# Zero products spread over the weight blocks, keys cast and transposed first in a step, and one copy for transposed keys: a change to a fused retention and feed-forward kernel

## The chip, the cores and the metric

The kernel runs on one core of a Trainium2 chip. The core has a matrix engine (TensorE, in the profile PE, with its weight loads as PEld), three engines that work on elements (VectorE or DVE, ScalarE or ACT, GpSimd or POOL), a sync engine (SP) that issues most transfers, and 16 DMA engines that carry them. The metric is the device time of one execution in microseconds; lower is better.

## What is computed

The reference has two stages. The first is a recurrence over 768 positions for 4 batches and 8 heads with head size 64, in which a state of 64x64 per head decays and takes up one outer product per position:

```python
for t in range(S):
    state = gamma * state + einsum('bhd,bhe->bhde', k[:, :, t], v[:, :, t])
    y[:, :, t] = scale * einsum('bhd,bhde->bhe', q[:, :, t], state)
x = y.transpose(0, 2, 1, 3).reshape(B * S, H * D)      # 3072 x 512
a, b = x @ w1, x @ w2                                   # 512 -> 1024
out = (a * b @ w3) @ w_out                              # 1024 -> 1024 -> 512
```

The inputs and the output are float32. The kernel computes its products in fp16 with sums in float32, and it folds w3 @ w_out into one matrix of 1024x512 before it needs it.

## The kernel before

**Tiles and steps.** The sequence is cut into chunks of 128 positions. One step handles one chunk of two batches, that is 256 rows of x; there are 12 steps (NSTEP = 12, numbered 0 to 11). Steps 0 and 1 are handled in another arrangement (pairs of positions), step 2 has its own function `step2` (line 844), and steps 3 to 11 run through `step(m)` (line 874). In each step, for all heads:

- `scores` (line 374) multiplies the transposed keys kT and the queries into psA, 32 small products; VectorE masks them into `am` (line 389).
- `intra` (line 521) multiplies `am` with the values into psY, and `inter` (line 590) adds the queries times the carried state.
- `kv` (line 537) multiplies keys and values into psK. VectorE adds the carried state to it (lines 572 and 564), and GpSimd decays the sum (line 565) to the state of the next chunk.
- `outputs_back` (line 606) scales psY into the tile `xt`, which is the input x of the feed-forward stage (line 613).

The class `Ffn` (line 621) holds the feed-forward stage. `ab(f)` makes one block of 128 of the 1024 hidden columns: eight products of 128x256 on TensorE (line 635), a copy of the first half's result by ScalarE (`pa`, line 644), and its product with the second half by VectorE (`ht`, line 650). `o_unit(e)` makes 128 output rows: eight products of 512 columns (line 660), a scaling by ScalarE into `osb` (line 664), and a store issued by the sync engine (line 666).

The stages are staggered. Step m computes the scores and the key-value products of chunk m, the outputs of chunk m-2 and the hidden columns of chunk m-1.

**What sets the order.** The schedule is written out by hand: each engine runs its instructions in the order in which the program emits them, and waits come only from data and from buffers. Transfers from the sync engine are one queue. The eight semaphores of this queue are taken in turn, so a transfer also waits until the transfer eight issues before it has landed. Buffers come from pools: the products of the feed-forward stage, psK and some transposes share four banks with the tag psF, `osb` has four buffers, kT two, k16 three.

**How the keys come.** `load_k(m)` (line 87) brings them into a staging tile, and is called two steps ahead. `k_cast` (line 295) turns them into fp16 in two halves, in `step` both on GpSimd (line 303). There are two ways to transpose them. `k_dma` (line 361) has the sync engine issue one transposing DMA from k16 to kT, for the keys of steps 5, 7, 8, 10 and 11. `k_transposes` (line 349) does it with eight products against an identity matrix on TensorE (line 357), for the keys of steps 2, 3, 4, 6 and 9; the result stands in one bank, and `cast_to` (line 216) copies one half to kT on VectorE (line 218) and the other on ScalarE (line 220). K_PE = (3, 5, 8) names the steps that prepare keys in this second way within `step`.

**The order within a step.** After `scores`, `inter` and `outputs_back` for the two sides, `step` emits the state's additions and decay (`kv_backs`), the masks (`am_back`), the first output unit with its store, then the key cast and the transposing DMA for the next step, then the second output unit with its store, and then the loads for later steps. The hidden columns, the value cast (`v_cast`, line 310) and, in even steps, the query casts and their transposing DMAs (`q_dma`, line 336) follow.

**The head.** At the start TensorE folds w3 and w_out block by block: `cast_w3` (line 227) casts a block of w3 as it lands, `w3_transpose` (line 240) transposes it with eight products and VectorE copies the result, `cast_wo` (line 222) casts a block of w_out on ScalarE and GpSimd, and `w3_part(f, i)` (line 250) adds two products of 512 columns per pair of blocks. `busy(m, tag, n)` (line 677) issues m products of a zero matrix with n columns (512 if none is given) whose result nobody reads; the kernel before does this eight times at the start and ten times with 84 columns after the first transposes.

Of the kernel before, what the change touches and what calls it, by code (L numbers as in the profile page):

```python
# [18 lines left out]
def kernel(  # L19
# [11 lines left out]
    nc = tc.nc  # L31
# [5 lines left out]
    NSTEP = (B // 2) * NCH  # L37
# [4 lines left out]
    K_PE = 4  # L42
# [173 lines left out]
    def cast_to(dst, src, on_dve):  # L216
        if on_dve:
            nc.vector.tensor_copy(dst, src)
        else:
            nc.scalar.copy(dst, src)  # L220

    def cast_wo(i):
        dst = WO[i][:, :, :].rearrange("p a n -> p (a n)")
        nc.scalar.copy(dst[:, 0:512], wo_st[i][:, 0:512])  # L224
        nc.gpsimd.tensor_copy(dst[:, 512:1024], wo_st[i][:, 512:1024])

    def cast_w3(f):
        t = att.tile([128, 1024], HP, tag="qT", name="w3h", bufs=5)
        st = w3_st[f]
        if f < 4:  # L230
            nc.vector.tensor_copy(t[:, 0:512], st[:, 0:512])  # L231
            nc.scalar.copy(t[:, 512:1024], st[:, 512:1024])
        else:
            cast_to(t[:, :], st[:, :], f == 4)
        W3h[f] = t

    def bank(tag, shape, dtype, name):
        return ps_at.tile(shape, dtype, tag=tag, name=name)

    def w3_transpose(f):  # L240
        src, ps = W3h.pop(f), bank(("X0", "X1")[f % 2], [128, 1024], HP, "psW3")
        for g in range(8):
            c0 = (g // 2) * 256 + g % 2
            nc.tensor.transpose(  # L244
                ps[:, g * 128 : (g + 1) * 128], src[:, c0 : c0 + 255 : 2], ident16[:, :]
            )
        w3t[f] = att.tile([128, 1024], HP, tag="k16" if f < 3 else "v16", name="w3t", bufs=3)
        nc.vector.tensor_copy(w3t[f][:, :], ps[:, :])  # L248

    def w3_part(f, *parts):  # L250

        for i in parts:
            for r in range(2):
                g = i * 2 + r
                nc.tensor.matmul(  # L255
                    acc[f], lhsT=w3t[f][:, g * 128 : (g + 1) * 128], rhs=WO[i][:, r, :],
                    start=(g == 0), stop=(g == 7),
                )
            if i == 3:
                cast_to(W3O[f][:, :], acc[f], f < 3)  # L260
# [19 lines left out]
    def q_cast(n, *engs):  # L280
        if n not in q_in:
            return
        q16s[n] = att.tile([128, 1024], HP, tag="q16", name="q16", bufs=2)
        pairs_cast(q16s[n], q_in.pop(n), *engs)
# [10 lines left out]
    def k_cast(m, engs):  # L295
        k16 = att.tile([128, 2, 512], HP, tag="k16", name="k16", bufs=3)
        k32 = k_in.pop(m)
        if len(engs) == 1:
            parts = [(k16[:, :, :].rearrange("p e x -> p (e x)"), k32[:, :, :].rearrange("p e x -> p (e x)"))]
        else:  # L300
            parts = [(k16[:, e, :], k32[:, e, :]) for e in range(2)]
        for eng, (dst, src) in zip(engs, parts):
            (nc.scalar.copy if eng is nc.scalar else eng.tensor_copy)(dst, src)  # L303
        k16s[m] = k16
# [40 lines left out]
    def new_kT(m):  # L345
        kTs[m] = att.tile([128, 2, NP, 128], HP, tag="kT", name="kT", bufs=2)
        return kTs[m]

    def k_transposes(m, tag, on_dve):
        k16, kT = k16s[m], new_kT(m)  # L350
        if tag:
            ps = bank(tag, [128, 2, NP, 128], HP, "psTk")
        else:
            ps = ps_f.tile([128, 2, NP, 128], HP, tag="psF", name="psTk")
        for e in range(2):
            for p in range(NP):
                nc.tensor.transpose(ps[:, e, p, :], k16[:, e, p * 128 : (p + 1) * 128], ident16[:, :])  # L357
        for e in range(2):
            cast_to(kT[:, e, :, :], ps[:, e, :, :], on_dve[e])

    def k_dma(m):
        nc.sync.dma_start_transpose(
            new_kT(m)[:, :, :, :].rearrange("p e a j -> p (e a) j"),
            k16s[m][:, :, :].rearrange("p e x -> p (e x)"),
        )
# [8 lines left out]
    def scores(m, engs=None):  # L374
        kT = kTs.pop(m)
        am = att.tile([128, 2, NP * 2, L], HP, tag="am", name="am")
        ps = [bank(f"X{r}", [128, NP * 2, L], FP, "psA") for r in range(2)]
        for e in range(2):
            for p in range(NP):
                for r in range(2):  # L380
                    for s in range(2):
                        nc.tensor.matmul(  # L382
                            ps[r][half(s), p * 2 + e, :], lhsT=kT[half(r), e, p, half(s)],
                            rhs=queries(m, e, p, s, r), start=True, stop=True,
                        )
        AMs[m] = am

        def back(r):
            nc.vector.tensor_tensor(  # L389
                am[:, r, :, :], ps[r][:, :, :],  # L390
                keep[:, :].unsqueeze(1).broadcast_to((128, NP * 2, L)), MULT,
            )

        return back
# [282 lines left out]
    def busy(m, tag="Y0", n=512):  # L677
        if tag:
            ps = bank(tag, [128, 512], FP, "psZ")
        else:  # L680
            ps = ps_f.tile([128, 512], FP, tag="psF", name="psZ")
        for _ in range(m):
            nc.tensor.matmul(ps[:, 0:n], lhsT=Z[:, 0:128], rhs=Z[:, 0:n], start=True, stop=True)
# [3 lines left out]
    acc = [ps_f.tile([128, DM], FP, tag="psF", name="psW")[:, :] for _ in range(4)]  # L687
    w3_transpose(0)
    cast_wo(0)
    busy(10, n=84)  # L690
    w3_part(0, 0)
    cast_w3(1)
    w3_transpose(1)
    cast_wo(1)
    w3_part(0, 1)
    w3_part(1, 0, 1)
    cast_w3(2)
    w3_transpose(2)
    cast_wo(2)
    w3_part(0, 2)  # L700
    w3_part(1, 2)
# [80 lines left out]
    def four_banks():  # L782
        return [ps_f.tile([128, 2, TB], FP, tag="psF", name="psF")[:, :, :] for _ in range(4)]
# [9 lines left out]
    ps = four_banks()  # L793
# [24 lines left out]
    ps = four_banks()  # L818
# [19 lines left out]
        f1.ab(f)  # L838
    q_transposes(3, "Y0", False)
    stores = [f0.o_unit(0, store=False)]  # L840
    k_transposes(2, "Y1", (True, False))
    f1.ab(2)

    def step2():
        am_back = scores(2)
        am_back(0)
        am_back(1)
        stores.append(f0.o_unit(1, store=False))
        k_cast(3, (nc.gpsimd, nc.scalar))
        for n in (4, 5):  # L850
            q_cast(n, nc.gpsimd)
        for n in (4, 5):
            q_dma(n)
        for store in stores:
            store()
        for f in range(3, 5):
            f1.ab(f)
        intra(2)
        kv_back = kv(2, True)
        kv_back(0)  # L860
        f1.ab(5)
        k_transposes(3, None, (True, False))
        f1.ab(6)
        kv_back(1)
        v_cast(3, (nc.gpsimd, nc.gpsimd))
        f1.ab(7)
# [5 lines left out]
    K_PE = (3, 5, 8)  # L872

    def step(m):

        kv_backs = []
        if m > 4:
            last = None if m in EARLY else ended(intra(m - 1))
            if m < NSTEP:
                kv_backs.append(kv(m, True))  # L880
                am_back = scores(m)
            inter(m - 1, last)
        else:
            inter(m - 1)
            if m == 4:
                kv_backs.append(kv(m, True))
            am_back = scores(m)
        outputs_back(m - 1, 0)
        outputs_back(m - 1, 1)
        if m >= NSTEP:  # L890
            return
        for kv_back in kv_backs:
            kv_back(0)
            kv_back(1)
        am_back(0)
        am_back(1)
        ffn[m - 2].o_unit(0)
        if m + 1 < NSTEP:
            k_cast(m + 1, (nc.gpsimd, nc.gpsimd))
            if m not in K_PE:  # L900
                k_dma(m + 1)
        ffn[m - 2].o_unit(1)
        load_q(m + 3) if m % 2 == 0 else None
        load_k(m + 2)
        load_v(m + 2)
        load_q(m + 3) if m % 2 else None
        for f in range(2):
            ffn[m - 1].ab(f)
        if m + 1 in EARLY:
            intra(m)  # L910
        if m + 1 < NSTEP:
            v_cast(m + 1, (nc.gpsimd, nc.gpsimd))
        if m == 3:
            intra(m)
            kv_back = kv(m)
            kv_back(0)
        ffn[m - 1].ab(2)
        ffn[m - 1].ab(3)
        if m == 3:
            kv_back(1)  # L920
        if m % 2 == 0:
            for n in (m + 2, m + 3):
                q_cast(n, nc.gpsimd)
            for n in (m + 2, m + 3):
                q_dma(n)
        for f in range(4, 8):
            if f == 6 and m in K_PE:
                k_transposes(m + 1, None, (True, False))
            ffn[m - 1].ab(f)

    step2()
# [40 lines left out]
```

## Time and profile before

| | us |
|---|---|
| median of 4 runs | 186.42 |
| lowest and highest | 185.82, 187.53 |
| the profiled execution | 186.32 |
| its span in the profile | 184.30 |
| TensorE busy | 174.8 (95%) |
| VectorE, ScalarE, GpSimd busy | 108.2, 74.5, 70.2 |
| products of the hidden columns (L635) | 672 of 128x256, 77.0 busy |
| products of the output units (L660) | 200, 43.7 busy |

The profile is one execution. Its page gives busy times by engine and by groups of instructions; other views give each engine's instructions in order of time, and for each idle time the instruction whose end released the waiting one. In a line of a timeline the first number is the start in us from the start of the span, the second the time from the first instruction's start to the last one's end, then engine, line, operation, output<-input by the program's names, shape and count; what stands in brackets is the idle time before it and its releaser. Products on TensorE overlap: a product that lasts 0.38 us alone follows its neighbour at a shorter pitch, so that a run of them lasts the count minus one times the pitch plus one whole duration. A row of SPq is the time that the sync engine took to issue a transfer; the transfer lands later.

### The profile page before, as it was taken

To read this page: it belongs to the slowest core of one execution; us is meant where nothing else is said; L and a number is where in the kernel's file an instruction comes from. 1 tells how busy PE (TensorE), PEld (TensorE's weight loads), DVE (VectorE), ACT (ScalarE), POOL (GpSimd) and SP (SyncE) were. 2 spreads that over 40 slices of the span, in tenths; PEclk is the share of its full clock that TensorE was granted. 3 is DMA by queue.
4 is the path that set the end of the run, shared out by engine and by line. 5 is a ranking of instruction groups with operands and counts; after the bars stand their busy time and mean duration, and the time that the engine had idled before them with its cause. 6 is when DMAs were issued, how large, how long until landed. Compare 5 with 4: busy or idle time off the path is not lost.

```text
span 184.3 us, 6239 instructions
## 1 busy us (share of the span) xinstructions
PE 174.8 (95%) x2642; PEld 125.2 (68%) x2642; DVE 108.2 (59%) x205; ACT 74.5 (40%) x161; POOL 70.2 (38%) x126
## 2 busy tenths in 40 slices
PE   7789979999989999999999999899999999999992
PEld 2545546688556785885967858669678587685872
DVE  1447667642559659648467584395585855846330
ACT  3445735655641342433344424233344242342532
POOL 3228355853447660924407365028253090000000
PEclk9999999999999999999999999999999999999999
DMA  6999999997899999999998999999998932200203
GB/s 210 406 413 391 292 289 358 410 351 178 179 250 233 191 268 215 241 270 211 157 253 199 241 221 205 188 240 275 195 134 215 190 80 68 105 9 13 104 0 114
DMA packets 78474, 39.44 MB, mean 214 GB/s; under 512 B 56304, under 2 KB 72944, under 8 KB 78448
## 3 DMA queue, kind: packets, MB, share of 16 engines
q1 hardware_dynamic: 78016, 38.54, 86.5%
q8 instruction: 20, 0.33, 0.8%
q10 hardware_dynamic: 432, 0.52, 0.8%
q14 instruction: 6, 0.05, 0.1%
HBM read 29.36 MB, written 6.29 MB: 193 GB/s over the span
## 4 chain that ended last, share of the span: by engine, by line
PE 60%; DMA 22%; SPq 9%; POOL 3%; ACT 2%; issue 1%; ACTq 0%; DVE 0%
PE psF L635 34%; PE psO L660 20%; SPq L63 9%; DMA stg<-in_k_dram 8%; DMA stg<-in_moe_w_out_dram 4%; DMA stg<-in_moe_w_dram 4%; DMA stg<-in_v_dram 3%; DMA kT<-k 3%; PE psY L598 2%; PE psY L530 2%; PE psA L382 1%; PE psK L550 1%; PE psTk L357 1%; POOL v L310 1%; ACT osb L664 1%
## 5 line engine op out<-in xcount | busy, mean ns | idle before, releaser
L635 PE MATMUL psF<-xt,w 128*128 128x256 f16 x672 | 77.0, 273 | 0.0
L635 PEld LDWEIGHTS <-w 128*128 128x128 f16 x704 | 68.2, 98 | 10.3
L650 DVE TENSOR_TENSOR ht<-pa,psF 128x256 f16<-128x256 f32 x88 | 36.9, 420 | 38.6 <-PE psF L635 21.8
L660 PE MATMUL psO<-w3o,ht 128*128 128x512 f16 (+2 forms) x200 | 43.7, 371 | 0.0
L644 ACT COPY pa<-psF 128x256 f32<-128x256 f32 x80 | 29.7, 372 | 33.8 <-PE psF L635 33.8
L660 PEld LDWEIGHTS <-ht 128*128 128x128 f16 x200 | 18.5, 98 | 19.7
L664 ACT ACTIVATE osb<-psO 128x512 f32<-128x512 f32 (+2 forms) x25 | 14.5, 580 | 41.4 <-PE psO L660 41.4
L613 DVE TENSOR_TENSOR xt<-psY,YS 64x512 f16<-64x512 f32 (+1 forms) x29 | 21.1, 727 | 5.7 <-PE psY L598 5.4
L310 POOL TENSOR_TENSOR v<-stg,VS 128x512 f16<-128x512 f32 x20 | 20.5, 1042 | 5.6 <-DMA stg<-in_v_dram 5.6
L565 POOL TENSOR_TENSOR t<-s,GS 128x512 f16<-128x512 f32 x8 | 8.3, 1039 | 37.2 <-DVE s L564 37.2
L290 POOL CAST q<-stg 128x1024 f16<-128x1024 f32 (+1 forms) x12 | 12.0, 1003 | 16.2 <-DMA stg<-in_q_dram 11.9
L389 DVE TENSOR_TENSOR am<-psA,keep 128x512 f16<-128x512 f32 x20 | 12.8, 680 | 0.7 <-PE psA L382 0.7
L303 POOL CAST k<-stg 128x512 f16<-128x512 f32 x18 | 10.7, 612 | 1.4 <-DMA stg<-in_k_dram 1.3
L255 PE MATMUL psW<-wo,w3t 128*128 128x512 f16 x32 | 7.8, 380 | 1.6 <-ACT wo L224 1.5
L787 PE MATMUL psF<-xt,w 128*128 128x256 f16 x64 | 8.5, 274 | 0.2
L248 DVE COPY w3t<-psW 128x1024 f16<-128x1024 f16 x8 | 5.5, 689 | 5.3 <-PE psW L244 5.3
L269 PE MATMUL psW<-wo,w3t 128*128 128x512 f16 x32 | 8.4, 381 | 0.0
L787 PEld LDWEIGHTS <-w 128*128 128x128 f16 x64 | 5.8, 98 | 2.0 <-ACT w L220 0.6
L572 DVE TENSOR_TENSOR t<-psK,t 128x512 f16<-128x512 f32 x9 | 6.2, 689 | 0.7 <-PE psK L550 0.5
L244 PEld LDWEIGHTS <-w3h 128*128 128x128 f16 x64 | 4.4, 103 | 3.0 <-DVE w3h L231 1.6
L382 PE MATMUL psA<-qT,kT 64*64 64x64 f16 x320 | 5.0, 195 | 1.4 <-DMA kT<-k 0.9
L255 PEld LDWEIGHTS <-w3t 128*128 128x128 f16 x32 | 3.0, 98 | 4.6 <-issue 1.7
(91 smaller groups left out, 150.4 us busy)
## 6 DMA issues: line engine op xcount, KB each, us to landing
stg<-in_moe_w_dram SPq DMA_DIRECT2D x16, 512.0 KB, 8.7
stg<-in_q_dram SPq DMA_DIRECT2D x12, 512.0 KB, 6.5
out_dram<-osb SPq DMA_DIRECT2D x22, 256.0 KB, 3.7
stg<-in_k_dram SPq DMA_DIRECT2D x20, 256.0 KB, 5.5
stg<-in_v_dram SPq DMA_DIRECT2D x20, 256.0 KB, 5.9
stg<-in_moe_w_out_dram SPq DMA_DIRECT2D x4, 512.0 KB, 6.8
stg<-in_k_dram SPq DMA_DIRECT2D x2, 512.0 KB, 10.1
stg<-in_v_dram SPq DMA_DIRECT2D x2, 512.0 KB, 8.9
```

Source lines behind the costliest of these rows:

```text
L63: nc.sync.dma_start(dst, src)
L255: nc.tensor.matmul(acc[f], lhsT=w3t[f][:, g * 128 : (g + 1) * 128], rhs=WO[i][:, r, :], start=(g == 0), stop=(g == 7),)
L290: (nc.scalar.copy if eng is nc.scalar else eng.tensor_copy)(dst[:, :].rearrange("i (t h d) -> i h t d", t=2, d=D)[:, hs, :, :], src[:, :]. ...
L310: eng.tensor_tensor(v16[:, e, :].rearrange("j (h d) -> j h d", d=D), v32[:, e, :].rearrange("j (h d) -> j h d", d=D), VS[:, 2, :].unsqueez ...
L389: nc.vector.tensor_tensor(am[:, r, :, :], ps[r][:, :, :], keep[:, :].unsqueeze(1).broadcast_to((128, NP * 2, L)), MULT,)
L613: nc.vector.tensor_tensor(XT[m][to, :, s, :].rearrange("p (a e) (i t) -> p a e t i", e=2, t=2), psYs[m][s][fr, :, :].rearrange("p (a e) (t ...
L635: nc.tensor.matmul(ps[:, :], lhsT=W[d][:, f * 128 : (f + 1) * 128], rhs=self.x(d), start=(d == 0), stop=(d == 3),)
L644: nc.scalar.copy(self.pa[f][:, :], ps[:, :])
L650: nc.vector.tensor_tensor(self.HT[:, f, :], self.pa.pop(f)[:, :], ps[:, :], MULT)
L660: nc.tensor.matmul(psO[:, :], lhsT=self.HT[:, f, e * 128 : (e + 1) * 128], rhs=W3O[f][:, cs], start=(f == 0), stop=(f == 7),)
L664: nc.scalar.activation(osb[:, cs], psO[:, :], AF.Copy, scale=final_scale)
L787: nc.tensor.matmul(ps[f // 2][:, f % 2, :], lhsT=W[d][:, f * 128 : (f + 1) * 128], rhs=f0.x(d), start=(d == 0 and f % 2 == 0), stop=(d == ...
```

## The change

It has three parts.

1. In the head, ten zero products of 84 columns after the first transposes become two of 400 columns. Three zero products of 512 columns are added after `w3_part(0, 0)`, three more after `w3_transpose(1)`, and two of 400 columns after `w3_transpose(2)`.
2. `k_transposes` copies the transposed keys with one VectorE copy of 1024 columns instead of one copy of 512 on VectorE and one on ScalarE.
3. In `step`, the key cast on GpSimd and, where the step is not in K_PE, the transposing DMA of the next step's keys move from behind the first output unit to right behind `outputs_back`. On GpSimd the cast is now ahead of the state's decay (L565); on the sync engine the transposing DMA is ahead of the first output unit's store. ScalarE, VectorE and TensorE keep their order apart from parts 1 and 2.

The parts of the diff (the same edit of the two other calls of `k_transposes` is left out):

```diff
-    def k_transposes(m, tag, on_dve):
+    def k_transposes(m, tag):
...
-        for e in range(2):
-            cast_to(kT[:, e, :, :], ps[:, e, :, :], on_dve[e])
+        nc.vector.tensor_copy(
+            kT[:, :, :, :].rearrange("p e a j -> p (e a j)"), ps[:, :, :, :].rearrange("p e a j -> p (e a j)")
+        )
...
     w3_transpose(0)
     cast_wo(0)
-    busy(10, n=84)
+    busy(2, n=400)
     w3_part(0, 0)
+    busy(3)
     cast_w3(1)
     w3_transpose(1)
+    busy(3)
     cast_wo(1)
     w3_part(0, 1)
     w3_part(1, 0, 1)
     cast_w3(2)
     w3_transpose(2)
+    busy(2, n=400)
     cast_wo(2)
     w3_part(0, 2)
...
-    k_transposes(2, "Y1", (True, False))
+    k_transposes(2, "Y1")
...
         outputs_back(m - 1, 1)
         if m >= NSTEP:
             return
+        if m + 1 < NSTEP:
+            k_cast(m + 1, (nc.gpsimd, nc.gpsimd))
+            if m not in K_PE:
+                k_dma(m + 1)
         for kv_back in kv_backs:
             kv_back(0)
             kv_back(1)
         am_back(0)
         am_back(1)
         ffn[m - 2].o_unit(0)
-        if m + 1 < NSTEP:
-            k_cast(m + 1, (nc.gpsimd, nc.gpsimd))
-            if m not in K_PE:
-                k_dma(m + 1)
         ffn[m - 2].o_unit(1)
```

More of the change, by code (lines that the diff above doesn't have):

```diff
@@ L861, in step2 @@
         f1.ab(5)
-        k_transposes(3, None, (True, False))
+        k_transposes(3, None)
         f1.ab(6)
@@ L927, in step @@
             if f == 6 and m in K_PE:
-                k_transposes(m + 1, None, (True, False))
+                k_transposes(m + 1, None)
             ffn[m - 1].ab(f)
```

## The prediction

> **What bounds the kernel now.** I read the page first, then the list of waits of TensorE, then the chain, then the engines' timelines around each wait.
>
> ```profile
> span 184.3 us, 6239 instructions
> PE 174.8 (95%) x2642; PEld 125.2 (68%) x2642; DVE 108.2 (59%) x205; ACT 74.5 (40%) x161; POOL 70.2 (38%) x126
> ...
> PE psW L255 <- ACT wo L224: 1.5, 2, 0.8
> PE psTq L328 <- DVE k L290: 1.2, 1, 1.2
> PE psA L382 <- DMA kT<-k: 0.9, 1, 0.9
> PE psA L382 <- ACT kT L220: 0.4, 1, 0.4
> PE psTq L328 <- POOL q L290: 0.3, 1, 0.3
> PE psW L244 <- DVE w3h L231: 0.2, 1, 0.2
> ```
>
> TensorE is busy for 95% of the span, and its work runs in one fixed order, so only two things change the time: a change of TensorE's own work after the head, or a change of the waits. The waits (total us, times, longest) are few. Three belong to the weight stage before 13 us, one (1.2) sits at 24.12, and 0.3, 0.4 and 0.9 come after it. From 24 us on, a wait saved moves the end; before 24.12, a wait saved or added is taken up by the 1.15 us that TensorE idles there until a key load has landed and been cast.
>
> **Part 1, zero products between the first blocks.** The head, TensorE alone (start, us, then count after the x):
>
> ```profile
> 1.27 3.60 PE L683 MATMUL psZ<-zeros 128*128 128x512 f16 x8 [1.27 <-DVE zeros L143]
> 4.85 1.04 PE L244 MATMUL psW<-ident,w3h 128*128 128x128 f16 x8
> 5.68 0.91 PE L683 MATMUL psZ<-zeros 128*128 128x84 f16 x10
> 6.68 0.64 PE L255 MATMUL psW<-wo,w3t 128*128 128x512 f16 x2
> 7.50 0.62 PE L244 MATMUL psW<-ident,w3h 128*128 128x128 f16 x8 [0.19 <-DVE w3h L231]
> 8.93 1.45 PE L255 MATMUL psW<-wo,w3t 128*128 128x512 f16 x6 [0.81 <-ACT wo L224]
> 10.22 0.61 PE L244 MATMUL psW<-ident,w3h 128*128 128x128 f16 x8
> 11.49 1.46 PE L255 MATMUL psW<-wo,w3t 128*128 128x512 f16 x6 [0.66 <-ACT wo L224]
> ```
>
> The eight first products have a pitch of (3.60-0.63)/7 = 0.42 us (one alone lasts 0.63); the six at 8.93 have (1.45-0.38)/5 = 0.214 (one alone 0.38). The eight transposes shrink from 1.04 to 0.62. So TensorE doubled its rate between 5.7 and 7.5, although the page's granted clock reads 1.00 throughout: this row of the page does not show the early half rate.
>
> Ten products of 84 columns go (slow pitch (0.91-0.28)/9 = 0.07, together 0.70) and two of 400 come (0.42x400/512 = 0.33 each, 0.66): equal, and both lie in the time until w3_part(0,0) may start at 6.68. Three of 512 follow w3_part(0,0): 6.68+2x0.214 = 7.11, so they end at 7.75, and w3_transpose(1) starts 0.25 later than 7.50. Behind it wait its copy on VectorE (8.16, now about 8.43 to 9.12) and the parts of row 1. The next three run from 7.75+8x0.055 = 8.19 to 8.83, inside the 0.81 gap that ends at 8.93 with ScalarE's cast of W_out; w3_part(0,1) is not delayed, and w3_part(1) at 9.36 finds its copy done (9.12). The last two of 400 run from 10.66 to 10.99, inside the gap ending at 11.49. In all 1.61 us of zeros in 1.66 us of gaps (0.19+0.81+0.66). Cost 0; nothing gained either, since loads and casts set 8.93 and 11.49. Without that cover the price is the zeros' own time less the 1.15 at 24.12.
>
> [...] The trace has one moment, before 7.5. By the row the cost is 0. [...]
>
> **Part 2, one copy for the transposed keys.** Step 2's first keys (VectorE, then ScalarE, then TensorE):
>
> ```profile
> 50.30 0.42 DVE L218 COPY kT<-psTk 128x512 f16<-128x512 f16 x1 [2.27 <-PE psTk L357]
> 50.89 0.59 ACT L220 COPY kT<-psTk 128x512 f16<-128x512 f16 x1
> 50.77 0.32 PE L382 MATMUL psA<-qT,kT 64*64 64x64 f16 x16
> 51.53 0.32 PE L382 MATMUL psA<-qT,kT 64*64 64x64 f16 x16 [0.44 <-ACT kT L220]
> ```
>
> ScalarE's half is late, behind an output's scaling. The single 1024-wide copy has an exact row (a kT copy at 24.78: 0.69). It starts at 50.30 as now and ends 50.99, so all 32 scores start at about 51.04. The scores of later steps take 0.31 from first to last start, plus 0.1 to the next product: 51.45, where the output's products start at 51.78 now. Gain 0.33.
>
> The same copy in steps 2 (k3), 3, 5 and 8 adds 0.69-0.42 = 0.27 to VectorE and takes 0.58 from ScalarE. VectorE is tightest after 56.25, where it runs on without a gap to 61.56: xt is done at 60.5 for 60.24 (read at 61.32) and the masked scores at 61.83 for 61.56 (read at 63.07). Cover 0.8 and 1.2, cost 0. Elsewhere it idles 0.4 between products. In step 5 the bank of the transposes is now freed by VectorE (92.04+0.69 = 92.73; its next product comes at 93.33: no wait), and the second state bank waits for VectorE instead of for ScalarE's last pa (ends 93.78 after being pushed back by its kT copy). That third psK product now goes at 93.83 for 93.70: gain 0.13.
>
> **Part 3, cast and transposing DMA first in the step.** What happens in step 7 now (sync queue):
>
> ```profile
> 107.49 4.81 SPq L340 DMA_TRANSPOSE qT<-q  x2
> 112.39 0.53 SPq L666 DMA_DIRECT2D out_dram<-osb  x1
> 113.02 1.28 SPq L362 DMA_TRANSPOSE kT<-k  x1
> 114.40 0.54 SPq L666 DMA_DIRECT2D out_dram<-osb  x1
> ...
> 118.72 0.45 PE L382 MATMUL psA<-qT,kT 64*64 64x64 f16 x32 [0.90 <-DMA kT<-k]
> ```
>
> The keys' DMA lands 5.66 after issue, 0.9 late. The least gain is the swap with one store: issue at 112.40, landing 118.06, and 0.28 of the wait stays (gain 0.62). But the same move in step 6 acts first. There the casts stand on GpSimd behind the state product L565, which waits for VectorE until 98.0; so the kT issue is at 100.18, the second store at 101.51, and the loads behind it start at 102.09. The keys of step 7 were issued by 91.7 and take 4.7 (median of the two): 96.4, when GpSimd idles (7.93 before L565). Casts (1.17) to 97.6, kT issue (1.23) to 98.8, both stores to 99.9: the loads of step 6 start 2.1 earlier. Then step 7's q transposes shift from 107.49 to 105.4 and end at 110.3, kT is issued there, and it lands at 113.4 to 116.0 (3.1, the median landing, to 5.7). Needed at 117.82. I take the full 0.90.
>
> What it costs: two casts pass L565, so L565 (1.04) ends up to 1.2 later, 111.0 for 109.83 in step 7; its result is next read by L572 at 121.76. The value casts behind are not passed. On the sync queue kT passes one store (256 KB, 0.5 to issue), which starts up to 1.5 later; its osb is one of four, two per step, so it is reused two steps (24 us) later. If a key load landed late, GpSimd, the sync queue, the stores and the loads behind them would wait for it: in step 4 the keys, issued by 69.7 and landing 5.4 later, are cast by 75.4 to 76 as now. Steps 3, 5 and 8 have no kT DMA and their casts pass only GpSimd's L565.
>
> [...]
>
> **Sum.** 0.33+0.13+0.90 = 1.36. The profiled execution took 186.32 (span 184.30 and 2.02 around it): 184.96. It lies 0.10 under the median 186.42, so 185.1. Unknown: at 131.2 TensorE loses 0.25 to ScalarE's mark in step 9, whose release no view explains; 0 to 0.25 gain, I take 0, because the mark waits for TensorE and not for the copy.
>
> **Rivals.**
> A (0.60): as summed, 184.6 to 185.6.
> B (0.20): the wait for keys stays or moves. [...] then 0.9 is not saved and only 0.46 is: 186.0. Against it: 1.8 us of room even at the slowest landing.
> C (0.12): more goes: the 0.25 at 131.2, 0.27 at 47.47, and longer waits in the slower of the four runs (187.53): about 184.3.
> D (0.08), slower: [...] Then the zeros cost 6x0.42+0.66 = 3.2, TensorE has no gaps to hide them, and 3.2-1.15 = 2.0 reaches the end: 188.4 without, about 187.1 with the gains. It decides once the zeros' excess passes 1.15, so for a doubling after about 10 us. Against it: the trace has it before 7.5, and the four runs lie within 1.7.
>
> **Numbers.** 185.1 is A's. The range 184.3 to 186.7 holds A, B and most of C, and leaves D's bad end out. One per cent of 186.42 is 1.86, about what a measurement can tell from no change: faster than 184.56 is C and A's lowest end, 0.15; slower than 188.28 is D's bad half, 0.05; the rest 0.80.
>
> **What would show it.** Right: no wait of psA for kT by DMA or ScalarE; the kT issue of step 7 before 111 and landed before 117; step 6's loads at about 100; the psK after step 5 within 0.3 from first to last start; w3_part(0,1) at 8.9 and (0,2) at 11.5 with zeros filling the gaps. Wrong: w3_part(0,2) after 12, products of 0.42 pitch past 8, a gap at 24.12 that has vanished, GpSimd waiting for a key load with the sync queue standing still, or psF waiting on VectorE's kT copy.

## The result, and the profile after

| | before | after |
|---|---|---|
| median, us | 186.45 (58 runs) | 184.57 (39 runs) |
| lowest and highest | 185.16, 189.86 | 183.65, 187.00 |
| the profiled execution, us | 186.32 | 184.69 |
| its span, us | 184.30 | 182.7 |

After against before on the same chips: 0.9904, interval 0.9886 to 0.9921. That is 1.79 us less (1.47 to 2.13, taken from 186.45). The sum had 1.36, a ratio of 185.1/186.42 = 0.9929: the sign, the place and most of the size were right, and the gain is somewhat larger than forecast; 184.57 lies just past the lower end of rival A's band (184.6). The ratios leave out executions over 1.5% above the fastest of their kernel; the only profile of s7 is of such a one (188.42, mean clock 0.95), so its stretches are not compared and what is read from it is marked.

The page of after:

```profile
span 182.7 us, 6235 instructions
PE 176.1 (96%) x2642; PEld 125.5 (69%) x2642; DVE 109.2 (60%) x205; ACT 72.0 (39%) x156; POOL 70.9 (39%) x126
```

TensorE still has 2642 products and VectorE 205 instructions, while ScalarE has five fewer (161 before): the five second halves of the copies, 2.5 us of ScalarE's time, against 1.0 more on VectorE. TensorE is busy for 1.3 us longer (larger zero products) in a span that is 1.6 shorter, so what went were waits. TensorE's waits in after (total, times, longest):

```profile
PE psW L255 <- ACT wo L224: 0.5, 2, 0.3
PE psW L244 <- DVE w3h L231: 0.5, 1, 0.5
PE psA L383 <- DVE kT L358: 0.3, 1, 0.3
PE psY L599 <- issue: 0.2, 1, 0.2
PE psF L791 <- ACT w L766: 0.2, 1, 0.2
```

Against the list of before: the 0.9 for the keys' DMA is gone, and so are the 0.4 for ScalarE's half of kT, the 0.3 for a query cast, and the 1.2 for the key load at 24 us. With that the cover that the prediction counted on for the head is used up in this execution (0.08 idle is left there). A wait on VectorE's one copy (0.3) stands at step 2's scores. New is a 0.2 called "issue", in which TensorE waited for nothing that the profile shows.

The sync queue in steps 6 and 7 of after:

```profile
99.25 0.45 SPq L63 DMA_DIRECT2D stg<-in_q_dram  x1
...
105.39 4.79 SPq L340 DMA_TRANSPOSE qT<-q  x2
110.28 1.29 SPq L363 DMA_TRANSPOSE kT<-k  x1
111.67 1.01 SPq L667 DMA_DIRECT2D out_dram<-osb  x2
```

Step 6's loads start at 99.25 (102.09 before), the query transposes at 105.39 (107.49), and the keys of step 7 are issued at 110.28 (113.02), ahead of both stores. They land 3.4 us later, at 113.7, where before they took 5.7 and landed at 118.7. Step 8's scores need them at 116.85 and do not wait. What moved the queue is GpSimd, before and then after:

```profile
98.00 1.04 POOL L565 TENSOR_TENSOR t<-s,GS 128x512 f16<-128x512 f32 x1 [7.93 <-DVE s L564]
98.99 1.17 POOL L303 CAST k<-stg 128x512 f16<-128x512 f32 x2
```

```profile
93.72 0.61 POOL L303 CAST k<-stg 128x512 f16<-128x512 f32 x1 [4.87 <-DMA stg<-in_k_dram]
94.70 0.61 POOL L303 CAST k<-stg 128x512 f16<-128x512 f32 x1 [0.38 <-DMA stg<-in_k_dram]
97.21 1.04 POOL L566 TENSOR_TENSOR t<-s,GS 128x512 f16<-128x512 f32 x1 [1.89 <-DVE s L565]
```

The casts of step 6 no longer stand behind the state's decay; they run as soon as their load has landed. The other side of this is a new wait: over the whole span GpSimd now idles 24.0 us before casts of keys until loads land, where in before it idled 1.3.

Right behind step 8's scores something else stands, in TensorE's timeline:

```profile
117.17 0.30 PE L599 MATMUL psY<-qT,t 64*64 64x64 f16 x12
117.65 0.35 PE L599 MATMUL psY<-qT,t 64*64 64x64 f16 x20 [0.17 <-issue]
```

Twelve of 32 products run, TensorE stops, and the other twenty follow. No data is late. This stop takes back a third of what the keys gave in this one execution; the last section comes back to it.

The head of after, TensorE:

```profile
7.30 0.81 PE L684 MATMUL psZ<-zeros 128*128 128x512 f16 x3
8.62 0.62 PE L244 MATMUL psW<-ident,w3h 128*128 128x128 f16 x8 [0.51 <-DVE w3h L231]
9.08 0.81 PE L684 MATMUL psZ<-zeros 128*128 128x512 f16 x3
10.11 1.46 PE L255 MATMUL psW<-wo,w3t 128*128 128x512 f16 x6 [0.22 <-ACT wo L224]
11.85 0.50 PE L684 MATMUL psZ<-zeros 128*128 128x400 f16 x2
12.68 1.45 PE L255 MATMUL psW<-wo,w3t 128*128 128x512 f16 x6 [0.32 <-ACT wo L224]
```

The zeros run at the doubled rate ((0.81-0.38)/2 = 0.215 per product) and each group ends before TensorE's next own work is ready: 0.51, 0.22 and 0.32 of each gap remain. The second block of w3 was cast late in this execution (ScalarE starts at 8.13, before at 7.01), so everything here is 1.1 us later than in the profile of before. The sync queue shows the same landing: its eleventh transfer, which waits for the third, this block of w3, starts at 8.13 too (before at 7.01). In the kernels without the added zeros its transposes start between 7.50 and 8.64, so the load moves and not the zeros.

### The profile page after: what moved, and what is told of

It reads as the page before. It is cut to its first block, busy times and chain, and to the rows that moved or that the text cites. A ratio compares the mean times of both kernels' runs of the same rounds, so it can differ in the third digit from the quotient of the medians.

```text
span 182.7 us, 6235 instructions
## 1 busy us (share of the span) xinstructions
PE 176.1 (96%) x2642; PEld 125.5 (69%) x2642; DVE 109.2 (60%) x205; ACT 72.0 (39%) x156; POOL 70.9 (39%) x126
## 4 chain that ended last, share of the span: by engine, by line
PE 79%; DMA 9%; SPq 8%; ACT 1%; issue 1%; DVE 0%; ACTq 0%
PE psF L636 40%; PE psO L661 23%; SPq L63 8%; DMA stg<-in_moe_w_out_dram 5%; DMA stg<-in_moe_w_dram 4%; PE psF L791 4%; PE psY L531 2%; PE psY L599 2%; PE psA L383 2%; PE psG L636 2%; PE psK L551 2%; PE psTk L357 1%; ACT w L220 1%; PE psTq L328 0%; ACT osb L665 0%
## 5 line engine op out<-in xcount | busy, mean ns | idle before, releaser
L684 PE MATMUL psZ<-zeros 128*128 128x512 f16 (+1 forms) x18 | 6.6, 504 | 1.3 <-DVE zeros L143 1.3
L225 POOL CAST wo<-stg 128x512 f16<-128x512 f32 x4 | 2.5, 612 | 10.4 <-DMA stg<-in_moe_w_out_dram 10.4
```

## The experiments

The question put to the runs: do waits at three places (step 2's scores, the state bank of step 6, the keys of step 8) explain the gain, or does more change hands? Theory A is the prediction's sum. Against it stand B (the wait for the keys stays or moves), C (more goes, above all at the mark in step 9) and D (the zeros cost or save).

Four stretches carry the comparison. They are read from TensorE's timeline, from the first output product of a step to the next one: "step 2" lies between its two output units, and "5 to 6", "7 to 8" and "8 to 9" are whole steps. Ratios are against before on the same chip.

| kernel | ratio | interval | step 2 | 5 to 6 | 7 to 8 | 8 to 9 |
|---|---|---|---|---|---|---|
| before | 1 | | 3.86 | 12.56 | 12.81 | 12.47 |
| after | 0.9904 | 0.9886, 0.9921 | 3.50 | 12.43 | 12.15 | 12.34 |
| p1: zeros only | 0.9986 | 0.9964, 1.0009 | 3.72 | 12.56 | 13.00 | 12.45 |
| p2: copy only | 0.9941 | 0.9908, 0.9974 | 3.50 | 12.43 | 12.79 | 12.24 |
| p3: order only | 0.9923 | 0.9892, 0.9953 | 3.72 | 12.56 | 11.80 | 12.46 |
| p23: after without zeros | 0.9881 | 0.9839, 0.9923 | 3.50 | 12.43 | 12.43 | 12.27 |
| p23 again | 0.9904 | 0.9868, 0.9940 | 3.50 | 12.43 | 11.80 | 12.24 |
| s6: order in step 6 only | 0.9954 | 0.9919, 0.9990 | 3.73 | 12.56 | 11.79 | 12.47 |
| s7: order in step 7 only | 0.9957 | 0.9933, 0.9980 | not compared | | | |
| c3: after, DMA where it was | 0.9910 | 0.9876, 0.9944 | 3.49 | 12.43 | 11.79 | 12.25 |
| a9: after, split copy in step 8 | one execution | | 3.50 | 12.43 | 12.02 | 12.24 |
| z2: after, zeros doubled | 0.9976 | 0.9946, 1.0006 | 3.49 | 12.43 | 11.80 | 12.24 |
| n0: after, no zeros in gaps | 0.9960 | 0.9934, 0.9986 | 3.50 | 12.43 | 13.08 | 12.31 |
| after again | 0.9892 | 0.9843, 0.9940 | 3.50 | 12.44 | 12.59 | 12.24 |

### Each part alone: p1, p2, p3

p1 is before with the edit of the zeros alone.

```diff
-    busy(10, n=84)
+    busy(2, n=400)
     w3_part(0, 0)
+    busy(3)
     cast_w3(1)
     w3_transpose(1)
+    busy(3)
...
     w3_transpose(2)
+    busy(2, n=400)
```

> The kernel before with part 1 alone (the zero products). Theory of the prediction: the zeros fill gaps of equal length and what remains is taken up by the wait at 24 us, so 0.0 us against the kernel before (within 0.3). Rival: the measured gain of about 1.8 us is larger than the 1.4 of copy and order because the zeros also help (the fast rate of TensorE comes or stays more surely), so 0.3 to 0.6 faster. Second rival: zeros delay the head, 0.3 or more slower.

186.16 us, 0.9986 (0.9964 to 1.0009): from 0.67 saved to 0.17 lost, with nothing as a good fit. TensorE's list of waits still has the keys:

```profile
PE psA L382 <- DMA kT<-k: 1.1, 1, 1.1
```

p2 is before with the one copy alone.

```diff
-        for e in range(2):
-            cast_to(kT[:, e, :, :], ps[:, e, :, :], on_dve[e])
+        nc.vector.tensor_copy(
+            kT[:, :, :, :].rearrange("p e a j -> p (e a j)"), ps[:, :, :, :].rearrange("p e a j -> p (e a j)")
+        )
```

> The kernel before with part 2 alone (one copy for the transposed keys). Theory: 0.33 at step 2's scores and 0.13 at step 5's end, so 0.4 to 0.5 us faster; the profile has no wait of psA for ScalarE and psK in step 6 spans under 0.3 from first to last start. Rival: VectorE's longer queue gives part of it back, 0.2 or less.

186.06 us, 0.9941 (0.9908 to 0.9974). Step 2 is 0.36 shorter than in before (0.22 than in p1 and p3, whose copies are two as well), step 6 is 0.13 shorter, and step 9 is 0.23 shorter: 0.58 to 0.72 together. The wait for the keys stays (0.9, once). For step 6, the copies in step 5 and the products of psK that wait behind ScalarE, in before and then in after (p2 has the same durations):

```profile
92.04 0.42 DVE L218 COPY kT<-psTk 128x512 f16<-128x512 f16 x1
92.50 0.58 ACT L220 COPY kT<-psTk 128x512 f16<-128x512 f16 x1 [0.97 <-DVE kT L218]
92.98 0.80 ACT L644 COPY pa<-psF 128x256 f32<-128x256 f32 x2
93.68 0.59 PE L550 MATMUL psK<-v,k 64*64 64x64 f16 x32
```

```profile
91.38 0.69 DVE L358 COPY kT<-psTk 128x1024 f16<-128x1024 f16 x1
93.02 0.45 PE L551 MATMUL psK<-v,k 64*64 64x64 f16 x32
```

The products of psK take 0.14 less. The lines show one thing more, which the prediction had not seen: the two halves did not run side by side. ScalarE sat idle for 0.97 and began its half as soon as VectorE's had ended; so it is at all four later places of before (idle 0.97 to 1.93), and in p1, p3 and s6 at step 2 too (idle 0.31). Why it waited is not shown.

p3 is before with the moved lines alone.

```diff
         outputs_back(m - 1, 1)
...
+        if m + 1 < NSTEP:
+            k_cast(m + 1, (nc.gpsimd, nc.gpsimd))
+            if m not in K_PE:
+                k_dma(m + 1)
...
         ffn[m - 2].o_unit(0)
-        if m + 1 < NSTEP:
-            k_cast(m + 1, (nc.gpsimd, nc.gpsimd))
-            if m not in K_PE:
-                k_dma(m + 1)
```

> The kernel before with part 3 alone (cast and transposing DMA first in the step). Theory: the wait of 0.9 for the keys of step 8 goes, so 0.6 to 0.9 us faster; the loads issued in step 6 start about 2 us earlier in the step. Rival: this part brings more than the one wait, because in other executions other steps wait for keys too: 1.2 or more. Second rival: nothing, the wait only moves.

185.31 us, 0.9923 (0.9892 to 0.9953), and no wait for the keys' DMA. Of the four stretches only 7 to 8 changes by more than p1 shows as well, from 12.81 (13.00 in p1) to 11.80. That is 1.01, where the wait that the list named was 0.90. An 11.8 is what such a step without transposes on TensorE takes when nothing is late (4 to 5 takes 11.73 in before and after).

### Parts 2 and 3 without the zeros: p23, twice

p23 is after with the zeros of before; its edit against after:

```diff
-    busy(2, n=400)
+    busy(10, n=84)
     w3_part(0, 0)
-    busy(3)
...
-    busy(3)
...
-    busy(2, n=400)
```

> The whole change without part 1. Theory: the sum, 1.3 to 1.4 us faster than before (ratio about 0.9927), and equal to the whole change within 0.3. Rival that the zeros matter: only 1.3, half a microsecond behind the whole change's 1.8. Rival that order and copy bring more than the profile showed: 1.8, like the whole change.

> Copy and order without the new zeros, a second time on one chip with the whole change, to settle what the zeros bring. Theory: equal to the whole change within 0.3. Rival: 0.3 to 0.6 behind it.

184.58 us, 0.9881 (0.9839 to 0.9923), and 184.34, 0.9904 (0.9868 to 0.9940): the whole gain is there without the zeros. The four stretches of p23 again give 0.36+0.13+1.01+0.23 = 1.73, against 1.79 measured for after. The gain thus belongs to parts 2 and 3, and the traces say where it lies. The near agreement of 1.73 and 1.79 is in part luck: it holds for an execution in which nothing stops TensorE. The same four stretches give only 0.36+0.13+0.66+0.13 = 1.28 in after's own profile and 0.93 in after again, and how often such stops come is not known. The ratios of p2 and p3 by themselves add up to 2.5 us; their intervals (0.5 to 1.7 and 0.9 to 2.0) hold the traces' 0.6 to 0.7 and 1.0.

### Which step's move took the wait away: s6, s7, c3

s6 and s7 move the lines of one step only (shown for s6; s7 has 7).

```diff
         outputs_back(m - 1, 1)
...
+        if m + 1 < NSTEP and m == 6:
+            k_cast(m + 1, (nc.gpsimd, nc.gpsimd))
+            if m not in K_PE:
+                k_dma(m + 1)
...
         ffn[m - 2].o_unit(0)
-        if m + 1 < NSTEP:
+        if m + 1 < NSTEP and m != 6:
```

> The kernel before with cast and transposing DMA moved in step 6 alone. Theory: step 6's loads start about 2 us earlier in the step, step 7's query transposes and its key transpose follow, and TensorE's wait for the keys of step 8 is gone although step 7 itself is unchanged. Rival: the wait needs the move in step 7 and stays at 0.3 or more.

185.16 us, 0.9954 (0.9919 to 0.9990); 7 to 8 is 11.79. The sync queue of s6:

```profile
99.10 0.46 SPq L63 DMA_DIRECT2D stg<-in_q_dram  x1
...
110.48 0.53 SPq L666 DMA_DIRECT2D out_dram<-osb  x1
111.11 1.29 SPq L362 DMA_TRANSPOSE kT<-k  x1
```

The loads of step 6 start 3.0 earlier and the keys of step 7, still behind one store, are issued 1.9 earlier. They land in 3.7. No wait is left.

> The kernel before with cast and transposing DMA moved in step 7 alone. Theory of the prediction: only the swap with one store acts, so the keys of step 8 are issued about 0.6 us earlier (just behind the query transposes) and 0.2 to 0.4 us of TensorE's wait for them stays. Rival: the wait goes altogether here already.

185.33 us, 0.9957 (0.9933 to 0.9980), and the ratio is that of s6. The profile, of the long execution, has no wait for the keys' DMA: with step 6 as it was, they are issued at 113.2 and land in 3.2. So by the profiles each move alone takes the wait away, and the two are not gains that add up; the ratios alone could not settle it, since the two gains together (0.46% and 0.43%) are not far from p3's 0.77%. In s7's profile the issue is no earlier than in before (113.0), so what vanished there is the slow landing. The prediction had this case as its least gain (0.62, for the earlier issue alone), which was too careful. But the place against the store does not set the landing: behind a store the keys took 5.7 in before, yet 3.7 in s6 and 3.4 in c3, and ahead of both stores they took 3.2 in s7, yet 5.4 in after again. Which transfers held the keys up is not shown.

c3 is after with only the DMA put back behind the first store; the cast stays early.

```diff
         if m + 1 < NSTEP:
             k_cast(m + 1, (nc.gpsimd, nc.gpsimd))
-            if m not in K_PE:
-                k_dma(m + 1)
...
         ffn[m - 2].o_unit(0)
+        if m + 1 < NSTEP and m not in K_PE:
+            k_dma(m + 1)
```

> The whole change, but the transposing DMA stays behind the first output unit's store, as before; only the cast is early. Theory drawn from the runs so far: what blocked the sync queue in step 6 was the cast standing behind the state product, not the order against the store, so this keeps all or nearly all of the gain (within 0.3 of the whole change) and TensorE does not wait for the keys of step 8. Rival: the place ahead of the store is what counts, and 0.3 or more of the wait comes back.

184.39 us, 0.9910 (0.9876 to 0.9944), the same as after. The keys of step 7 are issued at 111.49 and land in 3.4. With the cast early, the place of the DMA in the sync queue makes no difference that these runs resolve (their intervals are 0.3 to 0.6 us to each side). What counted in step 6 of before was GpSimd: the casts stood behind the state product L565, and the sync queue, with all of step 6's loads, stood behind the casts.

### The mark of step 9: a9

a9 is after, but the keys for step 9 are copied by halves again.

```diff
     def k_transposes(m, tag):
...
+        if m == 9:
+            for e in range(2):
+                cast_to(kT[:, e, :, :], ps[:, e, :, :], e == 0)
+            return
```

> The whole change, but the keys that step 8 prepares are copied in halves by VectorE and ScalarE as before. Rival that the profiles so far suggest: ScalarE's half is what makes the mark late in step 9, so the mark is again released by psK, about 0.85 us after the first intra product instead of 0.57, and TensorE loses about 0.2 there; step 2's and step 6's gains stay. Theory of the prediction: the mark's lateness is not the copy's, and it stays at 0.57.

183.78 us in its one execution, so it has no ratio. The mark of step 9 on ScalarE, in before, in after, then in a9:

```profile
131.21 0.19 ACT L586 COPY mark<-zeros 1x1 f16<-1x1 f16 x1 [0.76 <-PE psK L550]
```

```profile
129.49 0.19 ACT L587 COPY mark<-zeros 1x1 f16<-1x1 f16 x1 [0.52 <-PE psY L531]
```

```profile
128.80 0.19 ACT L591 COPY mark<-zeros 1x1 f16<-1x1 f16 x1 [0.47 <-PE psY L535]
```

In the last two it is released by the product that it marks, 0.56 us after the first product of `intra`. In before, p1, p3 and s6 the release shown is psK (L550), and the mark comes 0.84 to 0.86 after. The stretch 8 to 9 follows it: 12.45 to 12.47 there, and 12.24 to 12.34 in every kernel with the one copy. a9 was to tell whether step 8's own copy delays the mark, and it does not: with the split back in that step, the mark stays early. The rival written down for a9 is thus out. The delay goes with part 2, since p2 alone takes it away; which of the four other places does it, and why psK releases the mark there, is open.

### More zeros, none, and after once more: z2, n0, after again

z2 doubles the zeros in the gaps.

```diff
     w3_part(0, 0)
-    busy(3)
+    busy(6)
...
     w3_transpose(1)
-    busy(3)
+    busy(6)
...
     w3_transpose(2)
-    busy(2, n=400)
+    busy(4, n=400)
```

> The whole change with the zero products in the gaps doubled (six, six, and four of 400). Theory: 1.6 us more zeros, of which the idle time left in the gaps (0.2 to 1.1 in the profiles so far) and the wait of up to 1.15 at 24 us take most; between equal and 1.0 us slower than the whole change. Rival that more zeros help the clock further: faster than the whole change.

185.84 us, 0.9976 (0.9946 to 1.0006): most of the gain is lost. Yet its profile (185.11) has the first output product of step 2 at 47.54 (after 47.66), and later stretches like those of p23 again. In that profile the doubled zeros delay `w3_part(0, 1)` by 0.2 (10.35 for 10.11); the next gap takes most of this back (`w3_part(0, 2)` at 12.77 for 12.68), and at 24 us TensorE no longer idles (0.08), as in after. A stop called "issue" for an output unit, 0.6 us long, accounts for part. Where the other runs of z2 lost their time cannot be read from one profile.

n0 takes all zeros behind the first eight away.

```diff
     cast_wo(0)
-    busy(2, n=400)
     w3_part(0, 0)
-    busy(3)
...
-    busy(3)
...
-    busy(2, n=400)
```

> The whole change with no zero product after the first eight (neither the two of 400 ahead of the first part nor those in the gaps). Theory of the prediction: 0, within 0.3 of the whole change, since the wait at 24 us takes up a late head. Rival from the two executions in which TensorE fell back to half rate near 10 us: the half rate shows in the profile (pitch 0.42 between 8 and 14 us, granted clock under 1), and the time is 0.3 or more behind the whole change.

185.95 us, 0.9960 (0.9934 to 0.9986). TensorE runs the head at half its rate from the first product to about 13.5 us (the second eight transposes in 1.03, the next six products in 2.72 for 1.46), but step 2's first output product starts at 48.06, only 0.4 behind after. The larger loss is in the list of waits:

```profile
PE psY L599 <- issue: 1.1, 1, 1.1
```

It lies in the stretch 7 to 8 (13.08). So n0's time is no measure of what the zeros are worth. Its head is a late doubling: no product before 13.4 ran at the doubled rate, with TensorE idle for 0.79, 1.07 and 0.42 in between. In p2, which has the ten zeros of 84 columns but none in the gaps, something else happened. The rate had doubled by 4.59 us (the first eight transposes take 0.62, in before 1.04) and fell back:

```profile
8.64 0.62 PE L244 MATMUL psW<-ident,w3h 128*128 128x128 f16 x8 [2.02 <-DVE w3h L231]
10.10 2.12 PE L255 MATMUL psW<-wo,w3t 128*128 128x512 f16 x6 [0.84 <-ACT wo L224]
```

After idle times of 2.02 and 0.84 the six products take 2.12 instead of 1.46. The same happened in p23 (0.89 and 0.83), but not in p23 again (1.76 and 0.84). The page's row of the granted clock tells the two cases apart, n0 first, then p2:

```profile
PEclk9999999999999999999999999999999999999999
PEclk9969999999999999999999999999999999999999
```

It shows the fallback and not the late doubling. Of the eight profiled executions without zeros in the gaps two fell back and one doubled late; of the six with them, none did either. The mean granted clocks on record for single executions widen this. It was 0.997 or more in 97 of 98 executions of the five kernels with zeros in the gaps; in the seven without, before among them, it was under 0.995 in 121 of 211. (In p2 and p23 the fallback makes a mean of 0.991.) That is what part 1 does in these runs: it keeps the rate. It brings little, since the head mostly has time to spare: within the kernels without the zeros, those slower-clocked executions were on average 0.4 us longer than the others, which over all executions is about 0.2, inside p1's interval.

> The whole change itself on the same chip as the three others. Theory: 1.4 faster than before by the prediction's sum; by the traces so far 1.5 to 2.0.

184.16 us, 0.9892 (0.9843 to 0.9940), as the first measurement. But its profiled execution took 185.28, and there the wait for the keys is back:

```profile
PE psA L383 <- DMA kT<-k: 1.0, 2, 0.7
```

Here the keys of step 7 were issued at 112.43 and landed in 5.4, at 117.8; the stretch 7 to 8 is 12.59 for 11.80, and 4 to 5 is 12.18 for 11.73. The sync queue is two to three us late from 66.5 on, where two stores took 3.0 to issue (0.9 in after). With the casts first, the lateness hands itself on: the key loads are issued late, so GpSimd's casts wait for them, and the transposing DMA, the stores and the next loads wait for the casts. In step 4, after and then after again:

```profile
73.15 0.61 POOL L303 CAST k<-stg 128x512 f16<-128x512 f32 x1 [0.43 <-DMA stg<-in_k_dram]
```

```profile
75.93 0.61 POOL L303 CAST k<-stg 128x512 f16<-128x512 f32 x1 [1.85 <-DMA stg<-in_k_dram]
```

This is the cost that the prediction described for a key load that lands late. Rival B's wait for the keys thus exists, in one of the profiles with early casts (1.0 in all). The runs of after spread from 183.65 to 187.00 without a clear gap; that this wait makes the long ones is not shown.

## Why the prediction was right, and which term was off

- **Part 1, cost 0: right.** p1 measures nothing and p23 has the whole gain. The times foretold for the zeros (8.9 and 11.5) were missed by 1.2, since the w3 block landed later, not because of zeros. For that reason two of its signs of being wrong show in after (`w3_part(0, 2)` after 12, and no idle time left at 24 us) although the cost is 0. The danger weighed there, as rival D, was a late doubling of TensorE's rate. No profile with zeros in the gaps shows one; n0, without them, does, at about 13.5. The danger that it did not name is the opposite one, a clock that falls back in the gaps, in 2 of 8 profiles without zeros. Rival D, a late doubling in the usual execution with a cost of about 2, is out.
- **Part 2 at step 2, 0.33: right.** The row it took from another step (0.69 for the 1024-wide copy) holds exactly:

```profile
50.03 0.69 DVE L358 COPY kT<-psTk 128x1024 f16<-128x1024 f16 x1 [1.82 <-PE psTk L357]
50.78 0.45 PE L383 MATMUL psA<-qT,kT 64*64 64x64 f16 x32 [0.34 <-DVE kT L358]
```

  All 32 scores start behind one wait, and the stretch is 0.22 to 0.36 shorter. ScalarE's half was late for the reason given, an output's scaling, only in before's profile; in p1 and p3 it waited for VectorE's half, and there the gain is the 0.22.
- **Part 2 in step 6, 0.13: right.** 12.43 for 12.56 in every kernel with the one copy, and in none without.
- **Part 3, 0.90: right, a little low.** 1.01 in p3. The path was the one foretold, through step 6's loads; but by the profiles either of the two moves does it alone, and the margin is not always kept (after again). Its sign "GpSimd waiting for a key load" shows in every profile of a kernel with the casts first in all steps, mostly at no cost to TensorE.
- **The mark, 0 taken from 0 to 0.25: this term failed.** "The mark waits for TensorE and not for the copy" read the releaser of one line as the whole cause. With the one copy the mark is on time, by a path that is not known, and step 9 gains 0.23, nearly the upper end. Rival C had this term right. C's other place, the 0.27 at 47.47, is gone from after too, but behind a head that moves by more than that from run to run.

By traces 0.36+0.13+1.01+0.23 = 1.73 instead of 0.33+0.13+0.90+0 = 1.36: of the 0.37 too little, 0.23 is the mark, 0.11 the keys' stretch, and 0.03 step 2.

## What to carry to other kernels

Where a queue stands still, look for the engine that feeds it: here two casts moved past one GpSimd product that waited for VectorE started every load of step 6 2.8 us earlier, and the order within the queue made no measured difference any more. The price is that the queue now waits for the load instead. Before a copy is split between two engines, look in the trace whether the halves run side by side: here they ran one after the other, 0.42 and then 0.58, where one copy of both takes 0.69, and ScalarE's half also delayed the work behind it in step 5. If a release can't be explained by a view, keep its whole bound in the forecast instead of its lower end, and when two moves may each lift the same wait, don't add them.

## What was not expected of the hardware

**TensorE stops where no wait is shown.** In these traces the stops come at the same counts of products rather than at the same work. Counted from the first product, after and p23 stop before product 1759 (0.37 and 0.64 from start to start, part of it named "issue"). n0, with ten products fewer ahead, stops before product 1759 too (1.28), which is ten products further on in its work. a9 has a shorter stop at 1759: the 32 products of `inter` around it take 0.68, where they take 0.43 to 0.47 in the ten traces that do not stop there. z2, with eight more ahead, stops before 736 (0.95) and 2015 (0.40).

What holds TensorE up at these counts is not shown, and no run changed only how many products stand ahead of a place. The counts still bear on n0 and z2: before and after both issue 18 zeros, n0 has ten fewer and z2 eight more, and the longest stop of each (1.28 and 0.95) stands at other work than the stop of after. Their slower times can therefore not be put down to the zeros' own time alone.
